# One core: attention's loads spread over a chunk, a selection matrix built on the chip, load rows of whole 64 bytes, the first chunks' exponents reordered

## The chip, the cores and the metric

The kernel runs on one core of one Trainium2 chip. The metric is device time in microseconds, and the time before is the median of three runs. A second, profiled execution of the same program gives the trace that the rows below are from.

## The reference

Three stages in a row: a gated linear attention over 768 steps (2 batches, 8 heads of 40), a mixture of 8 experts with the best 2 for each of 1536 tokens, and a two-layer network. All inputs and the result are float32. Cut to what matters:

```python
for t in range(S):                                     # attention, S = 768
    m_new = np.maximum(f_gate[:, :, t] + m, i_gate[:, :, t])
    f_stab = np.exp(f_gate[:, :, t] + m - m_new)
    i_stab = np.exp(i_gate[:, :, t] - m_new)
    m = m_new
    C = f_stab[..] * C + i_stab[..] * einsum('bhd,bhe->bhde', vt, kt)
    n = f_stab[..] * n + i_stab[..] * kt
    h = einsum('bhde,bhe->bhd', C, qt)
    y[:, :, t] = sigmoid(o_gate[:, :, t]) * h / max(abs(sum(n * qt)), 1)
# experts: x is (1536, 320)
noisy = x @ w_gate + log1p(exp(x @ w_noise)) * noise   # top 2 of 8, softmax of the two
out[tok] += w * (relu(x[tok] @ w1[e]) @ w2[e])         # w1 320x1024, w2 1024x320
# network
h = x @ w_in                                           # 320 -> 2048
out = (h * clip(h + 3, 0, 6) / 6) @ w_out
```

## The kernel before

The order of the work is written out by hand: each engine executes its instructions in the order in which the program gives them, and the loads are nearly all issued from SP, also in program order, so a load that has to wait holds back all that SP would issue after it.

**Attention** runs in 12 chunks of 64 steps. The exponents of the gates come first: a scan over time gives the running maximum `mt` (`scan`, L177), and `exponents` (L187) turns it into three bfloat16 parts that are written into the tile `RWG`, for chunks 0 and 1 and for 2 and 3 on 16 rows each (`first_exponents(0)` and `(1)`), for the others at once on 64 rows (`later_exponents`, L217, after `mt` was copied to another layout by a POOL transfer into `m64`). A bfloat16 tile `SEL` (128 x 8 x 2 x 64) holds a selection of rows and an identity; `expo` (L296) multiplies it with `RWG` on TensorE (PE) and ACT takes the exponential into `dd`; POOL then scales the keys with it (`kt`, L310). `cbt` is a small tile of constants in bfloat16, among them the identity that `warm` (L367) uses to keep PE busy on 512 columns.

One turn n of the loop (L1138) does, on PE: `inter(n)` (queries by the state `Sb`), `values(n)`, `state(n)`, `scores(n+2)`, the transposes of chunk n-1's result (`xpose`, L437, copied to `xT` by ACT), `expo(n+2)`, at some n `decays`, and the router's `logits(n-1)`, which need `xT`. DVE does `pmul(n+1)` (scores by `dd`), the new state, and the normalisation `norm_eg`, `norm_pv`; ACT the rest of it (`norm2`, 9 operations) and the output gates (`gate`, in two or three operations on two chunks). In turns 4 to 10 the steps of `route` (`go(r0)`, `go(r1)`) stand between them on DVE, which find the slots of the tokens; from them POOL gathers the first expert's tokens.

Loads of a turn: `load_qk(n+3)` (two halves of 192 KB), `load_kv(n+3)` (324 KB, tiles in four buffers), `load_on` (two chunks' output gates), the store `put(n-1)`, and in the turns that `WD` names a piece of expert weights (`w_load`, 512 or 640 KB, into one of four buffers of `RAW`). Each piece is later split into a high part by ACT (`w_hi`, turns in `WH`) and a low part by DVE (`w_lo`, turns in `WL`; for the third piece of an expert both parts go into one stacked tile, L693). `w_split` does the two and the next load; the list `WS` names the steps of the first units for it.

**The experts** are units of up to 416 tokens: 8 blocks f of L1 (8 matmuls, L937), relu on ACT, and L2 (L973 to L978), with a lag of two steps. `bg(i, f, ...)` and `bga` hang other work on step f of unit i. `xprep` turns gathered tokens into `XH` and `XL` (L874 to L877). The network's units follow the experts' in the same loop.

Of the kernel before, what the change touches and what calls it, by code (L numbers as in the profile page):

```python
# [25 lines left out]
NT = 12  # L26
# [8 lines left out]
RAWB = 4  # L35
WL = (0, 0, 0, 1, 1, 1)
WD = (0, 1, 1, 1, 0, 0, 1, 0, 1, 2)
WH = (0, 0, 1, 1, 1, 0, 0, 0, 1, 1)
SP = 4
SP2 = 4  # L40
SPI = 4
WARM = 8
XW = 384
# [3 lines left out]
VSPLIT = {}  # L47
WS = ((0, 2), (0, 3), (0, 4), (0, 5), (0, 7), (1, 2), (1, 3), (1, 4), (1, 6), (2, 1))
TROWS = CAP + 11 * 128
# [22 lines left out]
@with_exitstack  # L72
def mlstm_moe_mlp(ctx, tc, qk, kv, on, gf, gf4, sl, w1, w2, w_in, w_out, cf, cb, out):
    nc = tc.nc
# [13 lines left out]
    def bank(i):  # L88
        return (ps if i >= 4 else psd).tile([128, 512], F32, name=f"bank{i}")
# [19 lines left out]
    nc.sync.dma_start(gft, gf)  # L109
    cbt = const.tile([128, 528], BF, name="cbt")  # L110
    A.dma_start(cbt, cb)
# [3 lines left out]
    ltri, ones = cbt[:, 256:384], cbt[:, 384:512]  # L115
    sel16 = cbt[:, 512:528].rearrange("p (h b) -> p h b", b=B)

# [12 lines left out]
    def kv_part(n):  # L130
        kvt[n] = att.tile([128, H * (D + V1)], F32, name="kv", bufs=4)
        return kvt[n], kv[n]
# [5 lines left out]
    def load_kv(n, eng=nc.sync):  # L138
        eng.dma_start(*kv_part(n))
# [13 lines left out]
    load_qk(0, (A, nc.sync))  # L153
    nc.sync.dma_start(SEL, sl)
    load_kv(0, A)
# [21 lines left out]
    def scan(a, b):  # L177
        V.tensor_tensor_scan(mt[:, a + 1:b + 1], gft[:, 1, a:b], gft[:, 0, a:b], mt[:, a:a + 1] if a else neg, OP.add, OP.max)

    scan(0, 128)  # L180
# [43 lines left out]
    late = None  # L224
    cft = const.tile([128, 444], F32, name="cft")
    wgt = cft[:, 288:336].rearrange("p (k c) -> p k c", k=3)
# [102 lines left out]
    def inter(n, bp=5, two=itp):  # L329
        q = QK[n % 3]  # L330
        vv = kvt[n][:, DM:].rearrange("p (h d) -> p h d", h=8)
        pv = [t.rearrange("p (a c) -> p a c", a=4)
              for t in (bank(bp)[:, 0:4 * V1], wb[:, 320:320 + 4 * V1] if bp == 5 else bank(6)[:, 0:4 * V1])]
        it = two[:, :, 0:4 * V1].rearrange("p x (a c) -> p x a c", a=4)
        for p in range(4 if n else 0):
            for x in range(2):
                r = slice(64 * x, 64 * x + D)
                for b in range(B):
                    T.matmul(it[rows[b], x, p, :], q[r, p, 0, rows[b]], Sb[r, b ^ x, p, :], start=True, stop=True)
        y_ps[n] = (pv, it, vv)  # L340
# [18 lines left out]
    def values(n):  # L359
        pv, _, vv = y_ps[n]  # L360
        for p in range(4):
            for b in range(B):
                for x in range(2):
                    h, r = 4 * x + p, rows[b ^ x]
                    T.matmul(pv[x][rows[b], p, :], Pt[n][r, h, :], vv[r, h, :], start=True, stop=True)

    def warm(k):  # L367
        for _ in range(k):
            T.matmul(wb, identb, cbt[:, 0:512], start=True, stop=True)

# [62 lines left out]
    lgt, xT = {}, {}  # L433
    wb = bank(7)
    rt = {}
# [241 lines left out]

    def raw_load(src):
        j = len(loaded) % RAWB
        t = RAW[:, 1280 * j:1280 * j + 1280]  # L680
        for r0, r1, ap, w in src:
            o = t[r0:r1, 0:w]
            nc.sync.dma_start(o if len(ap.shape) == 2 else o.rearrange("p (f d) -> p f d", d=DM), ap)
        return t
# [115 lines left out]

    def w_load():
        if pos[0] < len(queue):
            loaded.append(raw_load(queue[pos[0]][0]))
            pos[0] += 1
# [309 lines left out]


    scan(128, S)
    G.dma_start(m64, bass.AP(tensor=mt.tensor, offset=mt.offset + 256, ap=[mt.ap[0], [128, 4], [1, 129]]))
    warm(WARM)
    expo(0)
    scores(0)  # L1120
    decays(0, 2)
    expo(1)
    scores(1)
    pmul(0)
    fe = first_exponents(1)
    next(fe)
    next(fe)
    pmul(1)
    for _ in fe:
        pass  # L1130

    def norm(n):
        norm_pv(n)
        norm2(n)
        if n:
            put(n)

    for n in range(NT - 2):  # L1138
        if n:
            pmul(n + 1)  # L1140
        if n == 1:
            norm(0)
        if n == 9:
# [3 lines left out]
        if n + 3 < NT:  # L1147
            load_qk(n + 3)
            load_kv(n + 3)
        if n in (0, 1, 3, 5, 7):  # L1150
            load_on(n + 2 + n % 2 if n else 2)
        if n > 1:
# [3 lines left out]
        if n and n % 2 == 0:  # L1156
            gate(n, 2)
        state(n)
        norm_eg(n)
        if n:  # L1160
            norm_pv(n)
        else:
            for _ in later_exponents():
                pass
        if n == 1:
            G.tensor_copy(adj, iota8)
            G.tensor_copy(iotab, iota128)
        for _ in range(WD[n] if n < len(WD) else 0):
            w_load()
        if n == 0:  # L1170
            for i in range(3):
                gate(0, i)
        elif n % 2:
            gate(n + 1, 0)
            gate(n + 1, 1)
# [3 lines left out]
        if n in (6, 8):  # L1179
            go(r0)  # L1180
        expo(n + 2)
        if n == 0:
            decays(2, 4)
        elif n in (2, 6):
            decays(n + 2, n + 6)
# [11 lines left out]
        if 4 <= n <= 8:  # L1197
            go(r0)
        w_hi(WH[n] if n < len(WH) else 0)
        w_lo(WL[n] if n < len(WL) else 0)  # L1200
# [68 lines left out]
    bg(0, 1, open_late)  # L1269
    for f in range(2):  # L1270
        bg(0, f, w_lo)
        bg(0, f, w_load)
    for f in (2, 4, 6):
# [86 lines left out]
def _arrays(inp):  # L1360
# [18 lines left out]
    kn, vn = [_np.concatenate([z[:, :, :4], _np.roll(z[:, :, 4:], 64, axis=1)], axis=2) for z in (kn, vn)]  # L1379
    kv = _np.concatenate([kn.reshape(NT, 128, -1), vn.reshape(NT, 128, -1)], axis=2)  # L1380
    on = nat(o)[:, :, halves].reshape(NT, 128, H * D).transpose(1, 0, 2)
# [23 lines left out]
    for r in range(48):  # L1405
        sel[r // 16 * 32 + r % 16, r % 2 * 4 + r % 8 // 2, r % 16 // 8] = 1.0
    sq = sel.copy()
    sq[:, 4:] = sel[:, 4:, ::-1]
    sl = sq[:, :, :, None] + mk[:, None, None, 64:]
    sl = sl.astype(ml_dtypes.bfloat16)  # L1410
    cb = _np.concatenate([cb, sel.reshape(128, 16).astype(ml_dtypes.bfloat16)], axis=1)
    ci = (_np.arange(NT)[None] * 128 + p[:, None]).astype(_np.int32)
    cf = _np.concatenate([cf, wg.reshape(128, 48), nz.reshape(128, 96), ci.view(_np.float32)], axis=1).astype(_np.float32)
    a = dict(qk=qk, kv=kv, on=on, gf=gf, gf4=gf4, sl=sl, w1=inp['moe_w1'], w2=inp['moe_w2'],
             w_in=bits(inp['moe2_w_in']).reshape(DM, 2, F).transpose(1, 0, 2).reshape(2 * DM, F), w_out=bits(inp['moe2_w_out']).reshape(2, 8, 128, DM).transpose(0, 2, 1, 3).reshape(256, 8 * DM), cf=cf, cb=cb)
# [17 lines left out]
```

## Time and profile before

| | |
|---|---|
| median of 3 runs | 507.71 us (507.58 to 509.29) |
| profiled execution: time | 507.86 us |
| profiled execution: span, first to last instruction | 506.1 us |
| PE busy | 479.2 us, 95% of the span, 4554 matmuls |
| PE weight loads | 437.5 us, 86% |
| DVE / ACT / POOL busy | 333.8 (66%) / 237.8 (47%) / 94.7 us (19%) |
| granted PE clock, mean | 0.919 |
| moved by DMA | 91.00 MB, 180 GB/s over the span |

The page of the profile gives busy times and shares over the whole execution; the stages differ, so stretches of it are read by windows. Attention takes about the first 90 us, the experts run to about 310 us and the network to the end. A row of the timeline says when an instruction, or a run of like ones, began, how long it took, on which engine and line, what it wrote and read, and in brackets how long the engine had been idle before it and what ended that. "issue" there means that nothing in the profile explains the wait. Rows of the DMA view count the packets that a queue began in a stretch.

### The profile page before, as it was taken

Reading aid. Unit: us, or ns where it says so; the run is one execution under the profiler, and the core shown is the slowest. Engines: PE = TensorE matmul, PEld = TensorE weight load, DVE = VectorE, ACT = ScalarE, POOL = GpSimd, SP = SyncE. Lnnn points to the kernel's source line nnn. Section 1 sums busy time; section 2 is a strip of 40 time slices with the busy share of each in tenths; the row PEclk is TensorE's granted clock in tenths of the full one; section 3 lists DMA queues with packets and bytes.
Section 4 is the critical chain, followed back from the end, with each engine's and each line's share of the span. In section 5 each row is a group of like instructions: output and inputs, shape, how many; then the busy total and the mean of one; then the engine's idle time right before and its main releaser. Section 6 shows DMA issues by size and latency. Waiting matters only on the chain. (4 is left out here: it accounts for less than half of the span.)

```text
span 506.1 us, 11541 instructions
## 1 busy us (share of the span) xinstructions
PE 479.2 (95%) x4554; PEld 437.5 (86%) x4554; DVE 333.8 (66%) x823; ACT 237.8 (47%) x495; POOL 94.7 (19%) x117
## 2 busy tenths in 40 slices
PE   5799897989999999999999999899999999999996
PEld 3587785889999999999999998788888989999995
DVE  6756787698658787878788863676885434353534
ACT  3677665355446454545454633555553334333331
POOL 3323122305032010202010024784001000000000
PEclk9555555699999999999999999999999999999999
DMA  8978673477827998979887694979214300020111
GB/s 202 264 214 225 179 204 132 130 221 239 262 82 278 282 310 261 337 248 310 259 297 229 216 305 137 301 213 275 104 53 116 145 1 0 1 52 1 27 27 52
DMA packets 41193, 91.00 MB, mean 180 GB/s; under 512 B 4817, under 2 KB 23505, under 8 KB 41137
## 3 DMA queue, kind: packets, MB, share of 16 engines
q1 hardware_dynamic: 34736, 69.52, 44.2%
q0 software_dynamic: 5728, 19.73, 12.8%
q10 hardware_dynamic: 672, 0.99, 0.7%
q8 instruction: 36, 0.59, 0.5%
q14 instruction: 21, 0.16, 0.1%
HBM read 67.42 MB, written 22.68 MB: 178 GB/s over the span
## 5 line engine op out<-in xcount | busy, mean ns | idle before, releaser
L952 DVE SCALAR_TENSOR_TENSOR r<-r,bank 128x512 f32<-128x512 f32 (+1 forms) x56 | 34.2, 610 | 84.2 <-ACT r L951 82.3
L951 ACT ACTIVATE r<-bank,cft 128x512 f32<-128x512 f32 (+1 forms) x56 | 35.0, 626 | 99.1 <-PE bank L937 86.7
L940 ACT ACTIVATE hb<-bank 128x416 fp32r<-128x416 f32 (+2 forms) x80 | 35.7, 446 | 90.0 <-PE bank L937 77.9
L937 PE MATMUL bank<-XH,SB 128*128 128x416 f32 (+3 forms) x280 | 75.8, 341 | 0.3 <-PEq L1037 0.3
L937 PE MATMUL bank<-XL,SB 128*128 128x416 f32 (+3 forms) x192 | 67.1, 349 | 1.6 <-DVE XL L876 1.6
L973 PE MATMUL bank<-SB,hb 128*128 128x320 f32 x192 | 62.3, 324 | 3.2 <-ACT hb L924 2.8
L973 PE MATMUL bank<-SA,hb 128*128 128x320 f32 x192 | 60.8, 317 | 0.0
L864 POOL DMA_INDIRECT XG<-Xd,idx x32 | 34.7, 1083 | 138.9 <-PE bank L874 108.5
L975 PE MATMUL bank<-SB,hb 128*128 128x320 f32 x192 | 59.9, 312 | 0.1
L975 PE MATMUL bank<-SA,hb 128*128 128x320 f32 x192 | 59.3, 309 | 0.1
L974 PE MATMUL bank<-SA,hb 128*128 128x320 f32 x192 | 59.2, 308 | 0.0
L974 PE MATMUL bank<-SB,hb 128*128 128x320 f32 x192 | 59.2, 308 | 0.0
L937 PEld LDWEIGHTS bank<-XH,SB 128*128 128x128 f32 x280 | 50.3, 188 | 4.6 <-issue 0.6
L937 PE MATMUL bank<-XH,SA 128*128 128x416 f32 (+2 forms) x200 | 51.3, 329 | 0.0
L973 PEld LDWEIGHTS bank<-SB,hb 128*128 128x128 f32 x192 | 36.2, 188 | 5.3 <-ACT hb L924 3.8
L937 PE MATMUL bank<-XL,SA 128*128 128x416 f32 (+2 forms) x120 | 39.4, 329 | 0.2 <-DVE XL L876 0.2
L937 PEld LDWEIGHTS bank<-XL,SB 128*128 128x128 f32 x192 | 36.2, 188 | 3.9 <-DVE XL L876 1.9
L937 PEld LDWEIGHTS bank<-XH,SA 128*128 128x128 f32 x200 | 36.5, 196 | 1.6 <-ACT XH L875 0.3
L975 PEld LDWEIGHTS bank<-SB,hb 128*128 128x128 f32 x192 | 36.0, 188 | 1.4 <-DVE hb L925 1.3
L973 PEld LDWEIGHTS bank<-SA,hb 128*128 128x128 f32 x192 | 36.1, 188 | 1.1
L974 PEld LDWEIGHTS bank<-SA,hb 128*128 128x128 f32 x192 | 36.2, 188 | 0.9
L946 DVE SCALAR_TENSOR_TENSOR hb<-bank,hb 128x32 fp32r<-128x32 f32 x64 | 12.0, 188 | 37.6 <-ACT hb L940 37.5
(225 smaller groups left out, 1063.2 us busy)
## 6 DMA issues: line engine op xcount, KB each, us to landing
raw<-in_w_dram SPq DMA_DIRECT2D x18, 640.0 KB
raw<-in_w_dram SPq DMA_DIRECT2D x18, 512.0 KB
craw<-in_w_in_dram SPq DMA_DIRECT2D x8, 640.0 KB
craw<-in_w_out_dram SPq DMA_DIRECT2D x8, 640.0 KB
raw<-in_w_dram SPq DMA_DIRECT2D x18, 256.0 KB
qk<-in_qk_dram SPq DMA_DIRECT2D x23, 192.0 KB
Yd<-yo SPq DMA_DIRECT2D x24, 160.0 KB
kv<-in_kv_dram SPq DMA_DIRECT2D x11, 324.0 KB
```

The lines of the kernel that those rows point to most:

```text
L864: G.indirect_dma_start(out=XG[0:n, (u.xo + i) % 4, :], out_offset=None, in_=Xd[0:CUT[u.i] * 128] if early else Xd[:, :], in_offset=bass.In ...
L937: T.matmul(p, a, b, start=(i == 0), stop=(i == 7))
L940: A.activation(hb[:, 0:N], p, AF.Relu)
L946: V.scalar_tensor_tensor(hb[:, N:N + u.tail], p[:, o:N], 0.0, hb[:, o:N], OP.max, OP.subtract)
L951: A.activation(r, p, AF.Relu, bias=three)
L952: V.scalar_tensor_tensor(r, r, 6.0, p, OP.min, OP.mult)
L973: T.matmul(p, h, wh, start=s, stop=False)
L974: T.matmul(p, h, wl, start=False, stop=False)
L975: T.matmul(p, hb[:, lo:lo + n], wh, start=False, stop=t)
```

## The change

- `SEL` is no longer loaded (256 KB). Two pairs of matmuls on 512 columns build it in two banks, from the identity, 16 new columns of `cbt` and its 64-column identity, and ACT copies each bank to the tile. `warm` runs 4 times in place of 8, right behind them.
- Rows of `kv` go from 2592 to 2624 bytes, of `cbt` from 1056 to 1088, of `cft` from 1776 to 1792.
- `kv` has three buffers in place of four; `load_kv(n+3)` and `load_on` move from before `norm2` to behind `state(n)`.
- `w_load` moves to behind `expo(n+2)`, and a POOL memset of one element of the buffer stands before it, which the load has to wait for. `w_hi` moves from the end of a turn to before `state`. `WD`, `WH` and `WL` name other turns; one load comes in turn 9 ahead of the others, one behind the last chunk's normalisation.
- The scan is cut in two at step 256. Five steps of chunk 2 and 3's exponents go ahead of `pmul(0)`, the rest ahead of `pmul(1)`, and the scan of the remaining steps with the transfer to `m64` behind it. In turn 0 `norm_pv(0)` and `pmul(2)` come ahead of `later_exponents`.
- At the change to the experts, 3 and 2 warming matmuls are added around the first `xprep`, one `w_lo` goes ahead of unit 0, and one split goes from unit 0 to unit 1.

```diff
-WL = (0, 0, 0, 1, 1, 1)
-WD = (0, 1, 1, 1, 0, 0, 1, 0, 1, 2)
-WH = (0, 0, 1, 1, 1, 0, 0, 0, 1, 1)
+KW = 656
+WL = (0, 0, 0, 1, 1, 0, 0, 0, 1)
+WD = (0, 0, 1, 1, 0, 0, 1, 0, 1, 1)
+WH = (0, 0, 0, 1, 1, 0, 0, 1, 0, 1)
-WARM = 8
+WARM = 4
-WS = ((0, 2), (0, 3), (0, 4), (0, 5), (0, 7), (1, 2), (1, 3), (1, 4), (1, 6), (2, 1))
+WS = ((0, 2), (0, 3), (0, 4), (0, 6), (1, 0), (1, 2), (1, 3), (1, 4), (1, 6), (2, 1))
...
-    cbt = const.tile([128, 528], BF, name="cbt")
+    cbt = const.tile([128, 544], BF, name="cbt")
...
-    sel16 = cbt[:, 512:528].rearrange("p (h b) -> p h b", b=B)
+    sel16, selq = [cbt[:, c:c + 16].rearrange("p (h b) -> p h b", b=B) for c in (512, 528)]
...
-        kvt[n] = att.tile([128, H * (D + V1)], F32, name="kv", bufs=4)
+        kvt[n] = att.tile([128, KW], F32, name="kv", bufs=3)
...
     load_qk(0, (A, nc.sync))
-    nc.sync.dma_start(SEL, sl)
     load_kv(0, A)
...
+    for i in range(2):
+        p = bank(5 + i)
+        hs = slice(4 * i, 4 * i + 4)
+        T.matmul(p, identb, selq[:, hs, :, None].to_broadcast([128, 4, B, 64]), start=True, stop=False)
+        T.matmul(p, identb, eyeb[:, None, :].to_broadcast([128, 8, 64]), start=False, stop=True)
+        A.copy(SEL[:, hs].rearrange("p h b t -> p (h b t)"), p)
+    warm(WARM)
...
-    cft = const.tile([128, 444], F32, name="cft")
+    cft = const.tile([128, 448], F32, name="cft")
...
-    def raw_load(src):
+    def raw_load(src, held):
         j = len(loaded) % RAWB
         t = RAW[:, 1280 * j:1280 * j + 1280]
+        if held:
+            G.memset(t[0:1, 0:1], 0.0)
...
-    scan(128, S)
-    G.dma_start(m64, bass.AP(tensor=mt.tensor, offset=mt.offset + 256, ap=[mt.ap[0], [128, 4], [1, 129]]))
-    warm(WARM)
+    scan(128, 256)
     expo(0)
     scores(0)
     decays(0, 2)
     expo(1)
     scores(1)
+    fe = first_exponents(1)
+    for _ in range(5):
+        next(fe)
     pmul(0)
-    fe = first_exponents(1)
-    next(fe)
-    next(fe)
-    pmul(1)
     for _ in fe:
         pass
+    pmul(1)
+    scan(256, S)
+    G.dma_start(m64, bass.AP(tensor=mt.tensor, offset=mt.offset + 256, ap=[mt.ap[0], [128, 4], [1, 129]]))
...
     for n in range(NT - 2):
-        if n:
+        if n > 1:
             pmul(n + 1)
         if n == 1:
-            norm(0)
+            norm2(0)
...
             load_qk(n + 3)
-            load_kv(n + 3)
-        if n in (0, 1, 3, 5, 7):
-            load_on(n + 2 + n % 2 if n else 2)
         if n > 1:
             norm2(n - 1)
         if n:
             put(n - 1)
         if n and n % 2 == 0:
             gate(n, 2)
+        w_hi(WH[n] if n < len(WH) else 0)
         state(n)
+        if n + 3 < NT:
+            load_kv(n + 3)
+        if n in (0, 1, 3, 5, 7):
+            load_on(n + 2 + n % 2 if n else 2)
+        if n == 9:
+            w_load()
         norm_eg(n)
-        if n:
-            norm_pv(n)
-        else:
-            for _ in later_exponents():
-                pass
+        if n == 0:
+            for i in range(3):
+                gate(0, i)
+        norm_pv(n)
...
-        for _ in range(WD[n] if n < len(WD) else 0):
-            w_load()
-        if n == 0:
-            for i in range(3):
-                gate(0, i)
-        elif n % 2:
+        if n % 2:
             gate(n + 1, 0)
             gate(n + 1, 1)
...
         expo(n + 2)
+        for _ in range(WD[n] if n < len(WD) else 0):
+            w_load(True)
         if n == 0:
             decays(2, 4)
+            pmul(2)
+            for _ in later_exponents():
+                pass
...
-        w_hi(WH[n] if n < len(WH) else 0)
         w_lo(WL[n] if n < len(WL) else 0)
...
     norm(n)
+    w_load()
     norm_eg(n + 1)
     norm(n + 1)
     open_psd()
+    spare = bank(2)
+    warm(3, spare)
     xprep(units[0], 0, 5)
     xprep(units[0], 1, 3)
     xpose(n, 4)
+    warm(2, spare)
+    w_lo()
...
-    for f in range(2):
-        bg(0, f, w_lo)
-        bg(0, f, w_load)
+    bg(0, 0, w_load)
+    bg(0, 0, w_hi)
+    bg(0, 1, w_lo)
+    bg(0, 1, w_load)
```

## Rows read from the trace of the kernel before

**Rows 1.** Windows: busy us by engine (instructions), PE clock, DMA share, GB/s.
```profile
core 0: us, PE busy (x) PEld busy (x) DVE busy (x) ACT busy (x) POOL busy (x), PEclk, DMA share, GB/s
5.00:10.00 5.00, 4.09 (x63) 1.94 (x63) 3.24 (x9) 1.00 (x2) 0.54 (x1) 1.00 1.03 248
30.00:40.00 10.00, 10.00 (x316) 8.75 (x318) 5.24 (x14) 8.16 (x23) 2.27 (x3) 0.50 0.79 255
...
90.00:100.00 10.00, 9.77 (x95) 8.56 (x94) 6.18 (x15) 2.99 (x8) 3.96 (x7) 0.65 0.47 134
...
150.00:200.00 50.00, 50.00 (x313) 48.24 (x312) 40.62 (x82) 24.77 (x41) 8.09 (x8) 1.00 0.83 271
```

**Rows 2.** Timeline, PE, attention: start, length, what ran [idle before it].
```profile
21.76 0.80 PE L294 MATMUL s4p<-qk 40*64 40x64 f32 x18 [1.12 <-issue]
...
41.67 1.13 PE L294 MATMUL s4p<-qk 40*64 40x64 f32 x30 [1.15 <-issue]
...
76.77 0.48 PE L294 MATMUL s4p<-qk 40*64 40x64 f32 x3 [1.04 <-issue]
...
83.63 0.51 PE L349 MATMUL itp<-kv,kt 64*40 64x41 f32 x16 [1.71 <-issue]
```

**Rows 3.** Instruction queue: packets, MB, share; whole span, then 39.3:39.4, then 81.4:81.5.
```profile
q8 instruction: 36, 0.59, 0.5%
...
q8 instruction: 1, 0.02, 60.4%
...
q8 instruction: 1, 0.02, 60.3%
```

**Rows 4.** Timeline, SP's load issues in chunk 9.
```profile
77.13 0.87 SPq L683 DMA_DIRECT2D raw<-in_w_dram  x2
```

**Rows 5.** SP's load queue, 17.8 to 18.8 us: packets, MB, share of 16 engines.
```profile
q1 hardware_dynamic: 135, 0.31, 102.2%
```

**Rows 6.** Timeline, PE: inter of chunks 3 and 4.
```profile
31.71 1.36 PE L339 MATMUL itp<-Sb,qk 40*64 40x41 f32 x29
...
37.79 1.09 PE L339 MATMUL itp<-Sb,qk 40*64 40x41 f32 x32
```

**Rows 7.** DMA issues of the first 10 us: what, count, KB each.
```profile
SEL<-in_sl_dram SPq DMA_DIRECT2D x1, 256.0 KB
```

**Rows 8.** Timeline, PE, the head: warming and the first exponents.
```profile
3.94 3.60 PE L369 MATMUL bank<-cbt 128*128 128x512 bf16 x8 [3.94 <-DMA cbt<-in_cb_dram]
...
8.45 0.41 PE L300 MATMUL bank<-SEL,RWG 128*64 128x512 bf16 x2 [0.91 <-DMA SEL<-in_sl_dram]
```

**Rows 9.** Timeline, DVE and PE, chunks 5 and 6.
```profile
53.91 1.27 DVE L693 SCALAR_TENSOR_TENSOR SA<-sth,cft,raw 128x1024 fp32r<-128x1024 f32 x1
...
55.84 1.13 PE L294 MATMUL s4p<-qk 40*64 40x64 f32 x32 [1.45 <-DVE P L317]
```

**Rows 10.** Timeline, POOL, ACT and PE, chunk 3.
```profile
31.33 0.74 POOL L310 TENSOR_TENSOR kt<-kv,dd 128x320 f32<-128x320 f32 x1 [2.14 <-ACT dd L305]
...
31.54 1.05 ACT L687 CAST SA<-raw 128x1024 fp32r<-128x1024 f32 x1
...
34.51 0.73 ACT L147 ACTIVATE ont<-ont 128x640 f32<-128x640 f32 x1
...
36.33 0.48 ACT L442 COPY xT<-bank 128x384 f32<-128x384 f32 x1 [0.32 <-PE bank L440]
...
37.33 0.52 PE L453 MATMUL s4p<-cft,xT 128*32 128x16 f32 x24
```

**Rows 11.** Timeline, DVE and PE, chunk 10 and the first gathered tokens.
```profile
83.51 0.43 DVE L593 TENSOR_TENSOR yo<-yo,cft 128x256 f16<-128x256 f16 x1
...
84.77 0.42 PE L604 MATMUL s4p<-yo,yo 128*128 128x32 f16 x8
...
89.48 1.56 PE L874 MATMUL bank<-cft,XG 128*128 128x128 f32 x6
```

**Rows 12.** Timeline, PE, the first L1 of unit 1.
```profile
111.40 0.39 PE L937 MATMUL bank<-XL,SB 128*128 128x256 f32 x1 [1.63 <-DVE XL L876]
```

More of the change, by code (lines that the diff above doesn't have):

```diff
@@ L72, in mlstm_moe_mlp @@
 @with_exitstack
-def mlstm_moe_mlp(ctx, tc, qk, kv, on, gf, gf4, sl, w1, w2, w_in, w_out, cf, cb, out):
+def mlstm_moe_mlp(ctx, tc, qk, kv, on, gf, gf4, w1, w2, w_in, w_out, cf, cb, out):
     nc = tc.nc
@@ L178, in scan, with warm @@
         V.tensor_tensor_scan(mt[:, a + 1:b + 1], gft[:, 1, a:b], gft[:, 0, a:b], mt[:, a:a + 1] if a else neg, OP.add, OP.max)
+    wb = bank(7)
+    def warm(k, p=None):
+        for _ in range(k):
+            T.matmul(wb if p is None else p, identb, cbt[:, 0:512], start=True, stop=True)
+    for i in range(2):
[5 more added lines that the diff above has]
+    warm(WARM)
     scan(0, 128)
@@ L330, in inter @@
         q = QK[n % 3]
-        vv = kvt[n][:, DM:].rearrange("p (h d) -> p h d", h=8)
+        vv = kvt[n][:, DM:DM + H * V1].rearrange("p (h d) -> p h d", h=8)
         pv = [t.rearrange("p (a c) -> p a c", a=4)
@@ L365, in values @@
                     T.matmul(pv[x][rows[b], p, :], Pt[n][r, h, :], vv[r, h, :], start=True, stop=True)
-    def warm(k):
-        for _ in range(k):
-            T.matmul(wb, identb, cbt[:, 0:512], start=True, stop=True)
     xt, yt = {}, {}
@@ L433, in mlstm_moe_mlp @@
     lgt, xT = {}, {}
-    wb = bank(7)
     rt = {}
@@ L799, in mlstm_moe_mlp, with w_load @@
     pos = [0, 0]
-    def w_load():
+    def w_load(held=False):
         if pos[0] < len(queue):
-            loaded.append(raw_load(queue[pos[0]][0]))
+            loaded.append(raw_load(queue[pos[0]][0], held))
             pos[0] += 1
@@ L1379, in _arrays @@
     kn, vn = [_np.concatenate([z[:, :, :4], _np.roll(z[:, :, 4:], 64, axis=1)], axis=2) for z in (kn, vn)]
-    kv = _np.concatenate([kn.reshape(NT, 128, -1), vn.reshape(NT, 128, -1)], axis=2)
+    kv = _np.concatenate([kn.reshape(NT, 128, -1), vn.reshape(NT, 128, -1), _np.zeros((NT, 128, 8), _np.float32)], axis=2)
     on = nat(o)[:, :, halves].reshape(NT, 128, H * D).transpose(1, 0, 2)
@@ L1408, in _arrays @@
     sq[:, 4:] = sel[:, 4:, ::-1]
-    sl = sq[:, :, :, None] + mk[:, None, None, 64:]
-    sl = sl.astype(ml_dtypes.bfloat16)
-    cb = _np.concatenate([cb, sel.reshape(128, 16).astype(ml_dtypes.bfloat16)], axis=1)
+    cb = _np.concatenate([cb] + [z.reshape(128, 16).astype(ml_dtypes.bfloat16) for z in (sel, sq)], axis=1)
     ci = (_np.arange(NT)[None] * 128 + p[:, None]).astype(_np.int32)
-    cf = _np.concatenate([cf, wg.reshape(128, 48), nz.reshape(128, 96), ci.view(_np.float32)], axis=1).astype(_np.float32)
-    a = dict(qk=qk, kv=kv, on=on, gf=gf, gf4=gf4, sl=sl, w1=inp['moe_w1'], w2=inp['moe_w2'],
+    cf = _np.concatenate([cf, wg.reshape(128, 48), nz.reshape(128, 96), ci.view(_np.float32), cf[:, :4]], axis=1).astype(_np.float32)
+    a = dict(qk=qk, kv=kv, on=on, gf=gf, gf4=gf4, w1=inp['moe_w1'], w2=inp['moe_w2'],
              w_in=bits(inp['moe2_w_in']).reshape(DM, 2, F).transpose(1, 0, 2).reshape(2 * DM, F), w_out=bits(inp['moe2_w_out']).reshape(2, 8, 128, DM).transpose(0, 2, 1, 3).reshape(256, 8 * DM), cf=cf, cb=cb)
```

## The prediction

> **What bounds the kernel now.** The windows come first [rows 1]: TensorE (PE) is busy all 10 us of 30 to 40 and all 50 us of 150 to 200, so the kernel is PE-bound. But the granted clock is 0.50 (1.2 GHz) in the one and 1.00 (2.4 GHz) in the other. It is 1.00 in 5 to 10, and 0.65 over 90 to 100, where it comes back. Attention, about 15 to 90 us, runs at the low level, and PE fills even that. A microsecond gained or lost on PE before the experts start moves everything behind it, since nothing there is full except PE. So I list what PE waits for in attention.
>
> The timeline of PE has gaps put down to nothing ("issue"), the four longest of 1.12, 1.15, 1.04 and 1.71 us [rows 2]. The instruction queue explains them. Its 36 packets are 16 KB each, and PE runs 4554 matmuls with as many weight loads: 9108 / 36 = 253 instructions to a packet. Counted along the kernel, the gaps lie at multiples of about that. The packets that begin in the tenths at 39.3 and 81.4 us last 0.97 and 0.96 us (60.4% and 60.3% of 16 times 0.1 us) [rows 3], and PE resumes at 41.67 and 83.63: 1.4 and 1.3 us behind their ends. The later one begins only when two weight loads issued at 77.13 [rows 4] have drained. So a packet of code waits behind loads in flight, and PE stops if that takes longer than its last 250 instructions. Four smaller stalls only stretch a group of matmuls: 29 take 1.36 us in chunk 3, where chunk 4's 32 take 1.09 [rows 6]; by the same reading they come to 1.25 us.
>
> **The change, part by part.** The profiled execution took 507.86 us (span 506.1 and 1.8 around it), 0.15 above the median, 507.71. The sum starts from 507.86.
>
> *SEL made on the chip.* This removes a 256 KB load [rows 7] at the head of the queue. Loads run at 248 GB/s with the DMA engines full in 5 to 10 us [rows 1], so all behind it lands 0.262 MB / 248 GB/s = 1.06 us earlier, the code packet that ends the gap at 21.76 too. The first exponents wait 0.91 us for SEL [rows 8]. Four new matmuls of 512 columns take the place of four of the eight warming ones, at 0.45 us each (3.60 / 8), so PE's early activity and its instruction count stay; two ACT copies of about 0.6 us fall before RWG is ready. Take -1.05; ends 0 (something else, such as the output gates, lands last) and -1.5.
>
> *Exponents in another order.* The scan is cut, and chunk 2's exponents go ahead of pmul(0). That frees expo(2), but PE next meets a code boundary, which goes by the loads. In return norm_pv(0) and pmul(2) stand on DVE ahead of later_exponents, behind gates that ACT does when their load has come. Chunk 2's inter has some 4 us of slack over Sb. Take 0, ends -0.4 and +1.
>
> *Rows of whole 64 bytes.* In 17.8 to 18.8 us, mostly rows of kv, 0.31 MB moved at a share of 1.022, 303 GB/s [rows 5]. Full engines in 150 to 200 move 271 / 0.83 = 326. If the longer rows reach that, a load of 0.33 MB gains 0.08 us, and four of them in the head 0.3. Take 0, ends 0 and -0.3. The Trainium skill (DMA: Bandwidth & Descriptors, How a descriptor splits into AXI transactions) says that transactions start at 256-byte boundaries, so 2624-byte rows are cut up no better than 2592; by that it is 0 as well, and no row of before shows an aligned kv.
>
> *Loads spread out.* kv moves behind state and a weight load behind expo, held by a POOL memset that runs after kt. On SP the memset's wait stands ahead of the next chunk's qk, whose use is over 6 us away. Following the code boundaries (PE's order is kept) with the new issue times, most packets are asked for when little is queued. The one that ends at 41.67 still meets a weight load, qk and kv. I take the four small stalls and 0.15 of 1.15: -1.4; ends 0 and -2.4.
>
> *Conversions moved.* The stacked piece's subtraction (1.27 us on DVE) leaves the end of chunk 5, where it stood ahead of the pmul that held PE for 1.45 us [rows 9]. Take -1.2. It now stands at the end of chunk 8.
>
> w_hi moves from a chunk's end to its middle, and here ACT can be late: each piece is converted one chunk after its load was let go. In chunk 3, kt ends at 31.33 + 0.74 = 32.07 [rows 10]. Two loads from 77.13 drained by 81.4, so one takes half of 4.3 us, and some 1.2 more until it can be used: 3.0 to 3.3. ACT then converts at 35.1 for 1.05, does two gates of 0.74, and copies xT in 0.48: 38.1, where PE took the logits at 37.33. That is 0.8 late. Chunk 7 repeats it (0.9), chunk 4 has no gates there (0.1). Take +1.8; ends 0 and +8.9.
>
> *The last two chunks.* Gaps of 1.04 and 1.71 us go by the queues. But next is DVE: routing's one-hot product ends at 83.94, and PE takes it at 84.77 [rows 11], so only 0.83 is free, and the subtraction moved to chunk 8 adds 1.27 to this chain. With chunk 9's own slack I keep -0.3; ends -2.75 and +0.5.
>
> *Warming at the units' start.* Five matmuls of 0.45 us are 2.25. Three stand where PE would wait for the gather (4.3 us lie between the one-hot product's end and the first gathered tokens [rows 11], and PE's work between is 2.7 us), so nothing; two delay the first unit by some 0.4, since XL is late there anyway. In return the clock may rise sooner: in 90 to 100 it averages 0.65, that is, 7 us at half speed. Take -0.2; ends +1.7 and -1.7.
>
> *Splits moved in unit 0.* One w_lo goes ahead of unit 0, and one split behind unit 1's XL, each up to 1.48 us on a DVE that is full there. The 1.63 us that PE waits for XL [rows 12] should go: -1.5, ends 0 and -1.63.
>
> Sum: -1.05 - 1.4 - 1.2 + 1.8 - 0.3 - 0.2 - 1.5 = -3.85, so 504.0 us.
>
> **Rivals.** *The conversion waits for nothing*, and the code packets all get through: -1.8, -1.0 for the gap at 41.67 and -0.8 more in the last chunks: 500.4. For it speaks that a load by itself meets an empty queue in chunk 3.
>
> *The code gaps stay*, because loads are no less dense where packets are asked for, or because they are not the cause: the terms -1.4 and -0.3 fall away, 505.7. Against it stands that PE resumes at nearly the same distance behind both packets. The Trainium skill (Runtime: NRT & Kernel Launch, Instruction fetch mechanics) has code fetched in 16 KiB blocks with the cost "mostly hidden". The trace agrees on the block and not on the hiding: 1.71 us.
>
> *Slower: ACT stands behind a weight load.* In order, it holds the gates, xT and dd behind a w_hi whose piece has not come. If a held load needs 5 us from POOL's release, because it shares the queue with qk and kv, chunks 3, 4 and 7 lose 2.8, 2.0 and 3.0 us, and chunk 9 loses 1.1 beyond what DVE's chain hides: 8.9 in place of 1.8, 511.1. It decides from about 4.3 us on (no gain left); over 0.5% slower from 4.9. For it: two loads together took 4.3 us to drain. Against: in chunks 3 and 7 the queue should be empty.
>
> **How the numbers follow.** Forecast 504.0 (own range 502.3 to 505.2): 0.47. All gaps gone: 0.18. Gaps stay: 0.25. ACT behind the loads: 0.10. A measurement can tell about 0.5% from no change, so faster is below 505.2 and slower above 510.2. Faster: 0.44 of the forecast, 0.18, and 0.07 from the gaps that stay, where other terms do better: 0.69. Slower: 0.10, same: 0.21. The range, 500.3 to 507.8, leaves out the slow rival and the far ends of the gain.
>
> **What would show it.** The wait for SEL is gone and the gap of 21.76 ends near 20.7; the gaps at 76.77 and 83.63 are gone, with a wait for DVE in the place of the second; no 1.45 us wait in chunk 6, none for XL at unit 1. ACT's conversion in chunks 3 and 7 begins on a DMA, and logits there wait for xT. The prediction is wrong if ACT never waits for raw, if gaps stand behind code packets as before, or if the clock falls or rises at another place.

## The result and the profile after

The changed kernel is slower: 510.02 us median against 507.39 for the kernel before in the same session, ratio 1.0075 (95% interval 1.0052 to 1.0098). Forecast were 504.0 us and a range of 500.3 to 507.8. The profiled execution took 513.24 us (span 511.4), 3.2 above its median, so its waits are read for where they lie; what they are worth is read from ratios of medians. Executions of one kernel spread by about 1% to either side, and chips differ too (the kernel before had medians from 503 to 507.5), so every ratio below is to the kernel before on the same chip.

The timeline of PE in the kernel after (start, length, what ran, idle before it and its cause; P is what `pmul` writes on DVE, the scores times `dd`):

```profile
7.39 0.41 PE L314 MATMUL bank<-SEL,RWG 128*64 128x512 bf16 x2
12.00 0.50 PE L363 MATMUL itp<-kv,kt 64*40 64x41 f32 x30 [1.15 <-DVE P L331]
...
20.74 0.79 PE L308 MATMUL s4p<-qk 40*64 40x64 f32 x17 [1.47 <-issue]
27.30 1.14 PE L308 MATMUL s4p<-qk 40*64 40x64 f32 x32 [0.72 <-DVE P L331]
39.20 0.52 PE L462 MATMUL s4p<-cft,xT 128*32 128x16 f32 x24 [2.25 <-ACT xT L451]
46.33 0.38 PE L462 MATMUL s4p<-cft,xT 128*32 128x16 f32 x24 [1.47 <-ACT xT L451]
49.33 1.13 PE L308 MATMUL s4p<-qk 40*64 40x64 f32 x32 [1.21 <-DVE P L331]
69.08 0.53 PE L462 MATMUL s4p<-cft,xT 128*32 128x16 f32 x24 [3.72 <-ACT xT L451]
83.95 0.52 PE L462 MATMUL bank<-cft,xT 128*32 128x16 f32 x24 [2.29 <-ACT xT L451]
87.83 0.51 PE L363 MATMUL itp<-kv,kt 64*40 64x41 f32 x15 [1.15 <-issue]
```

Much of what the change was to remove is gone. The first exponents wait for no `SEL` and begin at 7.39, where [rows 8] had 8.45. Of the gaps of [rows 2], those at 41.67 and 76.77 are not there; the first ends at 20.74, near the 20.7 that was forecast, but is longer (1.47), and the last is 1.15. The 1.45 us wait for P of [rows 9] is gone, and one of 1.21 us stands a chunk earlier. What is new is that the logits wait for `xT` in chunks 3, 4, 7 and 9: 2.25 + 1.47 + 3.72 + 2.29 = 9.73 us, where [rows 10] shows none. In the timeline of ACT the cause stands ahead of the gates and the copy to `xT` each time:

```profile
36.33 1.04 ACT L698 CAST SA<-raw 128x1024 fp32r<-128x1024 f32 x1 [2.75 <-DMA raw<-in_w_dram]
44.86 1.04 ACT L698 CAST SA<-raw 128x1024 fp32r<-128x1024 f32 x1 [2.56 <-DMA raw<-in_w_dram]
66.21 1.04 ACT L703 CAST sth<-raw 128x1024 fp32r<-128x1024 f32 x1 [4.76 <-DMA raw<-in_w_dram]
80.87 1.26 ACT L698 CAST SA<-raw 128x1280 fp32r<-128x1280 f32 x1 [2.24 <-DMA raw<-in_w_dram]
```

The conversion of a weight piece (`w_hi`) waits for its load, and the gates and the copy to `xT` stand behind it in ACT's order. The loads' way to there, from the timelines of POOL and SP: the release and the issue for the pieces of chunks 3 and 7, and the issue alone for those of chunks 4 and 9:

```profile
31.92 0.09 POOL L691 MEMSET raw<- 1x1 f32 x1
32.04 0.33 SPq L694 DMA_DIRECT2D raw<-in_w_dram  x1
...
40.51 0.33 SPq L694 DMA_DIRECT2D raw<-in_w_dram  x1
...
59.74 0.09 POOL L691 MEMSET raw<- 1x1 f32 x1
59.85 1.22 SPq L694 DMA_DIRECT2D raw<-in_w_dram  x2
...
76.57 0.39 SPq L694 DMA_DIRECT2D raw<-in_w_dram  x1
```

From the issue on, ACT could begin after 36.33 - 32.04 = 4.3 us in chunk 3 and after 66.21 - 59.85 = 6.4 in chunk 7 (one piece in two transfers); the same subtraction gives 4.4 and 4.3 for the casts at 44.86 and 80.87.

### The profile page after: what moved, and what is told of

Same layout as the page of the kernel before. It is cut to its first block, busy times and chain, and to the rows that moved or that the text cites. A ratio compares the mean times of both kernels' runs of the same rounds, so it can differ in the third digit from the quotient of the medians.

```text
span 511.4 us, 11554 instructions
## 1 busy us (share of the span) xinstructions
PE 477.7 (93%) x4559; PEld 434.7 (85%) x4559; DVE 334.1 (65%) x824; ACT 238.4 (47%) x497; POOL 94.2 (18%) x122
## 5 line engine op out<-in xcount | busy, mean ns | idle before, releaser
L875 POOL DMA_INDIRECT XG<-Xd,idx x32 | 33.5, 1048 | 141.8 <-PE bank L885 110.1
L986 PEld LDWEIGHTS bank<-SA,hb 128*128 128x128 f32 x192 | 36.0, 188 | 1.5 <-DVE hb L954 1.1
L984 PEld LDWEIGHTS bank<-SA,hb 128*128 128x128 f32 x192 | 36.1, 188 | 1.1
L985 PEld LDWEIGHTS bank<-SA,hb 128*128 128x128 f32 x192 | 36.2, 188 | 0.9
```

What stands on the lines that cost most here:

```text
L875: G.indirect_dma_start(out=XG[0:n, (u.xo + i) % 4, :], out_offset=None, in_=Xd[0:CUT[u.i] * 128] if early else Xd[:, :], in_offset=bass.In ...
L984: T.matmul(p, h, wh, start=s, stop=False)
L985: T.matmul(p, h, wl, start=False, stop=False)
L986: T.matmul(p, hb[:, lo:lo + n], wh, start=False, stop=t)
```

## The experiments

Theory: what ACT waits for is the landing of a held load, and the other parts gain as forecast or less. Rivals: a cast in the middle of a chunk costs whether its load has come or not; or the waits only hide others.

**The conversion back at the turn's end** (kernel after, one line moved; label e1_hi_end).

```diff
-        w_hi(WH[n] if n < len(WH) else 0)
         state(n)
...
+        w_hi(WH[n] if n < len(WH) else 0)
         w_lo(WL[n] if n < len(WL) else 0)
```

> The kernel after, with one line moved back: each piece's conversion on ACT (w_hi) stands at the turn's end again, where the kernel before has it, ahead of w_lo. Loads, holds and all else stay as in the kernel after. Theory (ACT, in order, stands behind a held weight load, and PE waits for xT): the four waits of PE for xT in chunks 3, 4, 7 and 9 (2.25 + 1.47 + 3.72 + 2.29 = 9.73 us) go, some 1.5 us of it come back as waits for dd or P at the next turn's start, so about 8 us less than the kernel after: ratio to the kernel before 0.989 to 0.995. Rival (the order in the middle of a chunk costs by itself, the wait for raw only hides another wait, such as DVE's or a code packet's): the waits for xT get another name, and the ratio stays at 1.003 to 1.010.

Measured: 0.9965 (0.9940 to 0.9989), so 0.8 to 1.1% less than the kernel after with its two ratios, 1.0041 (below) and 1.0075; that is 4 to 5.5 us where 8 was expected. ACT waits for no raw in attention, PE for `xT` 0.4 us. Some of it came back as expected, as waits for P (4.65 us in sum against 3.68). In chunk 4 `w_lo` on DVE waits for the later cast, the next `pmul` stands behind it, and PE behind that:

```profile
45.23 1.23 DVE L699 TENSOR_TENSOR SA<-raw,SA 128x1024 fp32r<-128x1024 f32 x1 [1.75 <-ACT SA L698]
46.38 0.68 DVE L331 TENSOR_TENSOR P<-s4p,dd 128x512 f32<-128x512 f32 x1
...
47.12 1.13 PE L308 MATMUL s4p<-qk 40*64 40x64 f32 x32 [1.24 <-DVE P L331]
```

In this run the DMA view has the time from issue to landing (last column), which the page of the kernel before has not; for the four held pieces, let go in turns 2, 3, 6 and 8, and then for a load at the units' start:

```profile
raw<-in_w_dram SPq DMA_DIRECT2D x1, 512.0 KB, 4.2
raw<-in_w_dram SPq DMA_DIRECT2D x1, 512.0 KB, 5.4
raw<-in_w_dram SPq DMA_DIRECT2D x2, 256.0 KB, 3.9
raw<-in_w_dram SPq DMA_DIRECT2D x1, 640.0 KB, 5.3
...
raw<-in_w_dram SPq DMA_DIRECT2D x1, 512.0 KB, 4.0
```

Eight of the traces have landing times. Ahead of 100 us their weight loads took 3.5 to 6.3 us for 256 KB (these go out in pairs, and the median of a pair is given), 3.5 to 6.8 for 512 KB and 4.0 to 5.7 for 640 KB. So the size does not order them, and half the bytes do not land in half the time. How much is a fixed time and how much goes by the loads beside it, these rows do not tell apart.

**The conversion in the middle, in the kernel before** (the same line moved the other way; loads unheld, label e2_before_hi_mid).

```diff
+        w_hi(WH[n] if n < len(WH) else 0)
         state(n)
...
-        w_hi(WH[n] if n < len(WH) else 0)
         w_lo(WL[n] if n < len(WL) else 0)
```

> The kernel before, with only the conversion (w_hi) moved from a turn's end to its middle, ahead of state. Loads stay unheld and where they were. Theory (the wait is for the load, not for the place): in the kernel before a piece is asked for ahead of the gates of the turn before, so it has landed; ACT waits for no raw, and the time is that of the kernel before within 1 us: ratio 0.998 to 1.002. Rival (a cast of 1.04 us in the middle delays gates, xT and dd whether its load has come or not): five casts at 0.5 to 1 us each on PE's path, ratio 1.005 to 1.010, with waits of PE for xT or dd but none of ACT for raw.

Measured: 0.9996 (0.9972 to 1.0021). The theory's time holds, its "ACT waits for no raw" does not: even unheld, three of five pieces are late, by 0.9 to 1.8 us, and PE waits 1.85 us for `xT` in sum.

```profile
33.65 1.04 ACT L687 CAST SA<-raw 128x1024 fp32r<-128x1024 f32 x1 [0.96 <-DMA raw<-in_w_dram]
41.38 1.05 ACT L692 CAST sth<-raw 128x1024 fp32r<-128x1024 f32 x1 [1.76 <-DMA raw<-in_w_dram]
```

So the place of the cast alone costs nothing that can be told (some 1.2 us to either side); what costs is the place together with a load that comes late for it.

**Loads one turn earlier** (kernel after, conversions left in the middle; labels e4_loads_earlier and, on another chip, e9_loads_earlier).

```diff
-WD = (0, 0, 1, 1, 0, 0, 1, 0, 1, 1)
+WD = (0, 1, 1, 0, 0, 1, 0, 1, 1)
```

> The kernel after, with each held weight load of turns 2, 3, 6, 8 and 9 asked for one turn earlier (turns 1, 2, 5, 7, 8), at the same place in the turn; the conversions stay in the middle of turns 3, 4, 7 and 9. Theory (ACT stands behind the load, which took 4.3 to 6.4 us from POOL's release until ACT could begin): with some 6.4 us more in hand every piece has landed, ACT waits for no raw and PE for no xT; 7 to 9 us less than the kernel after, ratio 0.988 to 0.995. Rival (the conversion in the middle is the cost, not the load): ratio 1.003 to 1.010, PE still waits for xT or dd. If code gaps come back because loads are denser, one or two of about 1 us, that shows as issue gaps, not as waits for xT.

> The same kernel as e4 (the kernel after, held loads one turn earlier), again, beside the three edits of it that follow. Theory (what ACT waited for is gone, and the rest of the change gives 2 to 3 us): ratio to the kernel before 0.992 to 0.997, no wait of PE for xT over 0.6 us. Rival (the 0.9945 was a matter of that chip): ratio 0.997 or more.

Measured: 0.9945 (0.9922 to 0.9969) and 0.9959 (0.9929 to 0.9989). The four casts wait for nothing:

```profile
32.58 1.04 ACT L698 CAST SA<-raw 128x1024 fp32r<-128x1024 f32 x1
...
39.33 1.03 ACT L698 CAST SA<-raw 128x1024 fp32r<-128x1024 f32 x1
...
59.05 1.04 ACT L703 CAST sth<-raw 128x1024 fp32r<-128x1024 f32 x1
...
72.44 1.25 ACT L698 CAST SA<-raw 128x1280 fp32r<-128x1280 f32 x1
```

One tuple takes the change from 0.4 to 0.75% slower than the kernel before to about 0.5% faster, with the hold, and with the order of all work on ACT, unchanged.

**The kernel after again, and without the hold** (labels e5_after, e6_no_hold; same chip).

```diff
-            w_load(True)
+            w_load()
```

> The kernel after, unchanged, on the same chip as the next runs, so that what its waits for xT cost can be read against one set of runs of the kernel before. Theory (ACT behind the held loads): PE waits for xT in chunks 3, 4, 7 and 9 again, some 8 to 10 us in all, and the ratio to the kernel before is 1.005 to 1.010, that is 10 us of waits less some 6 us that the rest of the change and a clock that rises in the pauses give. Rival (the waits of the first trace were of that one execution): under 5 us of waits and a ratio under 1.003.

> The kernel after with the POOL memset ahead of the held loads left out (w_load(True) made w_load()): a load is issued where SP comes to it, behind kv of the same turn. In the trace of the kernel after SP had issued kv (and the gates) at 29.7, 35.4, 56.6 and the held load only at 32.0, 40.5, 59.9: 2.3, 5.1 and 3.3 us later. Theory (the landing takes 4 to 6 us wherever it starts, and the hold adds its wait to it): the loads land at about 35, 40.5 and 62 by the old times, ACT waits 0 to 1.5 us in each place, PE for xT 0 to 2 us in all; ratio 0.995 to 1.000. Rival (the queue is what is slow: unheld, a load only shares it with kv in place of qk and lands no earlier): ACT still waits 2 us and more in three chunks, ratio 1.003 to 1.010.

Measured: 1.0041 (1.0014 to 1.0069) for the kernel after, with waits of 1.74, 1.28, 3.28 and 4.30 us for `xT`, 10.6 in sum; 0.9966 (0.9941 to 0.9990) without the hold. Its first two loads go out at 29.34 and 35.47, and of the waits for raw (12.3 us in the kernel after) 3.5 us are left:

```profile
33.61 1.04 ACT L698 CAST SA<-raw 128x1024 fp32r<-128x1024 f32 x1 [0.48 <-DMA raw<-in_w_dram]
...
42.09 1.04 ACT L698 CAST SA<-raw 128x1024 fp32r<-128x1024 f32 x1 [2.25 <-DMA raw<-in_w_dram]
...
60.30 1.04 ACT L703 CAST sth<-raw 128x1024 fp32r<-128x1024 f32 x1 [0.76 <-DMA raw<-in_w_dram]
```

The piece of chunk 4 came later than expected: its load went out right behind kv's (34.55) and could be used 6.6 us after its issue (42.09 - 35.47), where the held one of the kernel after took 4.4. So the hold's 2 to 5 us are not all gained, but most are. With the conversion moved, the hold removed or the load advanced, one at a time, the loss goes; that settles the cause.

The two runs are from one chip, so their traces show what the waits for `xT` are worth. Ahead of unit 0 PE's waits of 0.15 us and more come to 18.0 us in e5 and to 10.2 in e6: 10.95 for `xT` (the four and one of 0.35) are gone, but 5.9 are put down to issue in place of 4.2, and 1.9 to other operands in place of 0.3. Of these 7.8 us unit 0 begins 4.2 sooner (91.69 for 95.92), close to the 3.8 of the ratio. Most of the rest had come back through the clock in e5: in 70 to 80 us 0.84 is granted (0.50 in e6), inter of 32 takes 0.68 us there in place of 1.09, and from 72.51 to 79.15 PE needs 4.9 us without its waits, where e6 needs 7.6 for the same groups.

```profile
73.61 0.68 PE L353 MATMUL itp<-Sb,qk 40*64 40x41 f32 x32
```

Whether the pauses bring the clock back is not shown; it is one execution of each.

**SEL alone** (kernel before with the matrix made on the chip and four warming matmuls fewer, label e3_sel; the edit is that of the change).

> The kernel before, with only the selection matrix made on the chip (four matmuls of 512 columns and two ACT copies, four warming matmuls fewer, no 256 KB load). Theory (the forecast's term): all loads of the head land 1.05 us earlier, the first exponents wait for no SEL, the gap of PE at 21.76 moves to about 20.7; ratio 0.997 to 0.999. Rival (another load or a code packet sets the head, and nothing is gained): ratio 1.000, with the gap of PE put at the same place or the time before it filled by another wait.

Measured: 0.9975 (0.9951 to 0.9999), 0 to 2.5 us, with the forecast's 1.05 in it. The wait for `SEL` is gone, but in this execution a gap of 1.68 us stands at 18.57 in place of the one at 21.76, and PE ran at the low level from the first exponents on, as the lengths of the rows show (the last section comes back to them):

```profile
7.65 0.64 PE L306 MATMUL bank<-SEL,RWG 128*64 128x512 bf16 x2
...
8.76 1.13 PE L300 MATMUL s4p<-qk 40*64 40x64 f32 x32
...
18.57 0.17 PE L255 MATMUL bank<-cbt,RWG 128*64 128x8 bf16 x1 [1.68 <-issue]
```

So this trace cannot show where the gap goes.

**Load rows alone** (kernel before with the padded rows, label e8_rows).

> The kernel before with only the load rows made whole multiples of 64 bytes (kv 656 in place of 648 columns, the two constant tiles 544 and 448). Theory (rows of 2624 bytes move no faster than 2592): kv lands as late as in the kernel before, within 0.2 us, ratio 0.999 to 1.002. Rival (whole 64-byte rows gain, up to the rate of full engines, 326 in place of 303 GB/s): 0.3 us at the head and shorter kv landings, ratio 0.998 to 0.9995.

Measured: 0.9984 (0.9957 to 1.0011). Both expectations lie in the interval and this trace has no landing times, so it stays open whether the rows gain 0.3 us or nothing.

**The exponents' order undone** (on the kernel with earlier loads, labels e7_exponents_undone and, beside e9, e12_exponents_undone).

```diff
-    scan(128, 256)
+    scan(128, S)
...
-    for _ in range(5):
-        next(fe)
     pmul(0)
-    for _ in fe:
-        pass
+    next(fe)
+    next(fe)
     pmul(1)
...
-            pmul(2)
```

> The kernel with the loads one turn earlier (e4), with the first chunks' exponents put back in the order of the kernel before (one scan from 128 on, pmul(0) ahead of them, norm of chunk 0 in turn 1, no pmul(2) ahead of the later exponents). Theory (the forecast's 0 for this part was too low a cost: PE's wait for P of 1.5 us in chunk 1 and 0.5 us in chunk 2 are the new order's): these fall to about 0.5 us in all, chunk 3 begins 0.5 to 1.5 us sooner, ratio 0.991 to 0.994 where e4 had 0.9945. Rival (the code gaps and chunk 2's slack take it, as forecast): chunk 3 begins within 0.4 us of e4's, ratio 0.994 to 0.996.

> The same kernel as e7 (e4 with the first chunks' exponents in the order of the kernel before), beside e9 this time. Theory (the new order costs PE 1 to 1.5 us of waits for P in chunks 1 and 2): waits for P before 30 us fall from 2.0 to about 0.5 us, ratio 0.001 to 0.003 below e9's. Rival (the waits are exchanged for a gap behind a code packet later in the same chunks, as e7's 3.12 us at 37.4 suggests): the sum of gaps put down to issue is 2 us and more above e9's, ratio equal to e9's or above it.

Measured: 0.9961 (0.9936 to 0.9987) and 0.9906 (0.9871 to 0.9941), with 0.9945 and 0.9959 for the other order: not told apart. In the traces the waits for P ahead of 30 us fall to 0.53, as the theory had it, and gaps put down to issue take their place, as the rival had it, for instance in e7:

```profile
12.24 0.50 PE L363 MATMUL itp<-kv,kt 64*40 64x41 f32 x30 [0.53 <-DVE P L331]
16.59 0.17 PE L263 MATMUL bank<-cbt,RWG 128*64 128x8 bf16 x1 [1.52 <-issue]
...
37.36 0.42 PE L316 MATMUL bank<-RWG,SEL 128*128 128x64 bf16 x5 [3.12 <-issue]
```

**No warming at the units' start** (e9 without its five matmuls, label e10_no_warm).

```diff
-    warm(3, spare)
...
-    warm(2, spare)
```

> e9 without the five warming matmuls at the units' start (three ahead of the first split, two behind the last transposes). Theory (forecast: they cost and give back about the same, -0.2 us): the first unit starts 0.5 to 1.5 us sooner and the granted clock rises up to 3 us later behind its start, ratio within 0.002 of e9's. Rival (the earlier rise of the clock is a gain of its own, since in the kernel before it came 5.4 us behind the unit's start and here 1.5 us): without them 1.5 to 2.5 us slower, ratio 0.003 to 0.005 above e9's.

Measured: 0.9954 (0.9928 to 0.9981), e9's ratio. Windows of 92 to 96 us, first with the warming (e9), then without:

```profile
92.00:94.00 2.00, 2.00 (x39) 1.83 (x38) 0.40 (x2) 1.57 (x3) 0.52 (x1) 1.00 0.86 260
94.00:96.00 2.00, 2.00 (x17) 2.00 (x16) 1.56 (x3) 0.38 (x2) 0.00 (x0) 1.00 0.45 108
```
```profile
92.00:94.00 2.00, 2.00 (x32) 1.74 (x32) 0.42 (x1) 0.69 (x2) 0.81 (x1) 0.50 0.44 152
94.00:96.00 2.00, 2.00 (x35) 1.84 (x34) 0.34 (x1) 1.63 (x3) 0.24 (x1) 0.76 1.07 275
```

The granted clock does rise some 4 us sooner, and the time is the same within the intervals.

**The first units' conversions undone** (e9 with the order of the kernel before in unit 0; labels e11_unit0_splits, e13_unit0_splits, and e14_both_undone with the exponents undone too).

```diff
-WS = ((0, 2), (0, 3), (0, 4), (0, 6), (1, 0), (1, 2), (1, 3), (1, 4), (1, 6), (2, 1))
+WS = ((0, 2), (0, 3), (0, 4), (0, 5), (0, 7), (1, 2), (1, 3), (1, 4), (1, 6), (2, 1))
...
+        if n == 9:
+            w_hi()
...
     warm(2, spare)
-    w_lo()
...
-    bg(0, 0, w_load)
-    bg(0, 0, w_hi)
-    bg(0, 1, w_lo)
-    bg(0, 1, w_load)
+    for f in range(2):
+        bg(0, f, w_lo)
+        bg(0, f, w_load)
```

> e9 with the conversions at the first units put back as in the kernel before: a fifth piece converted at the end of turn 9, no w_lo ahead of unit 0, unit 0's splits in the old list. Theory (the wait for XL at unit 1 was exchanged for waits behind the same full DVE): PE's wait for XL comes back at 1 to 1.6 us, the waits of 0.2 to 0.6 us for hb and yo between 100 and 125 us go, ratio within 0.002 of e9's. Rival (forecast: -1.5 us for this part): 1.5 us slower, ratio 0.003 above e9's, waits of PE in 100 to 125 us 1.5 us more in sum.

> The same kernel as e11 (held loads one turn earlier, the first units' conversions in the order of the kernel before), since its first ratio, 0.9895, had an interval of 0.0040 to either side. Theory (the new order of the conversions costs in unit 0, where a cast of 1.26 us stands on ACT ahead of an activation that PE and DVE go on from: from unit 0's first matmul to the first store of unit 3 e11's trace had 79.4 us, e4's and e9's 80.3 and 81.8): 79 to 80 us again, ratio 0.988 to 0.993. Rival (e11's were good executions, the two orders are alike): 80 to 82 us, ratio 0.994 to 0.997.

> e13 with the first chunks' exponents in the order of the kernel before as well, so that of the change there remain SEL on the chip, the load rows, the spread loads one turn earlier and the warming. Theory (both orders cost something: 1 us and more each): ratio 0.985 to 0.991, 0.002 to 0.004 below e13's, PE's waits for P before 30 us at 0.5 us. Rival (the exponents' order is exchanged for code gaps, as in e7 and e12, whose gaps of 2.15 and 3.12 us were put down to issue): ratio equal to e13's within 0.002 or above it.

Measured: 0.9895 (0.9855 to 0.9935), 0.9954 (0.9922 to 0.9985) and 0.9934 (0.9903 to 0.9966): all are faster than the kernel before, none is told from e9 by its time. The traces differ more clearly. From unit 0's first matmul to unit 3's first store e11 takes 168.31 - 88.93 = 79.4 us, e13 79.0 and e14 79.6; the eight traces with the new order and the warming take 79.7 to 82.2, 81.0 in the mean. The first two rows are e9's activations around the moved cast, the third is e11's:

```profile
92.02 1.26 ACT L698 CAST SA<-raw 128x1280 fp32r<-128x1280 f32 x1
93.18 0.39 ACT L951 ACTIVATE hb<-bank 128x256 fp32r<-128x256 f32 x1
```
```profile
92.61 0.38 ACT L951 ACTIVATE hb<-bank 128x256 fp32r<-128x256 f32 x1 [0.41 <-PE bank L948]
```

Counted from unit 0's first matmul the second relu is 4.0 us in for e9 and 3.7 for e11. PE's wait for XL falls (1.62 us in e11, 0.42 in e9), but others come up at once, here in e9 (`hb` is what relu writes):

```profile
109.59 0.41 PE L986 MATMUL bank<-SA,hb 128*128 128x320 f32 x1 [0.41 <-DVE hb L954]
110.98 0.35 PE L613 MATMUL bank<-yo,yo 128*128 128x32 f16 x8 [0.54 <-DVE yo L602]
113.45 0.42 PE L984 MATMUL bank<-SB,hb 128*128 128x320 f32 x1 [0.63 <-DVE yo L1017]
...
120.58 0.52 PE L885 MATMUL bank<-cft,XG 128*128 128x128 f32 x3 [1.66 <-DMA XG<-Xd,idx]
```

The longest is not one for DVE, but for gathered tokens (XG). It differs from execution to execution: none in e4, 1.71 us in e12, and with the old order none in e11 and e13, 0.64 in e14. All of PE's waits of 0.15 us and more in the stretch come to 2.0 to 3.9 us, mean 2.9, in the eight traces and to 1.9, 1.9 and 2.5 in the three; so they are somewhat under half of the difference in length, and the rest of it stays open.

## Why the prediction was wrong, step by step

**The conversions moved: mis-sized, and the cause of the sign.** The step had the mechanism: ACT in order, `xT` behind the held load, chunks 3, 4, 7 and 9. It took 3.0 to 3.3 us from POOL's release until the piece can be used; the trace shows 4.3 to 6.4. With these in place of 3.0 the step's own sum gives 2.1, 1.5 and 4.3 us of waiting in chunks 3, 4 and 7, and 2.25, 1.47 and 3.72 were measured; so it was this size that was off. The error is in the half: two loads issued together drained in 4.3 us [rows 4], and I gave one of them half. The same pair, issued at 77.01 in e3, whose trace has landing times, took 4.0 us from issue to landing in the median, and the first of the two 3.6:

```profile
raw<-in_w_dram SPq DMA_DIRECT2D x2, 512.0 KB, 4.0
```

So one of two takes nearly as long as the two together, and in the fuller chunks longer still. A page would have led to the same place: the Trainium skill (DMA: Bandwidth & Descriptors, Anatomy of one DMA) gives, for the gpsimd path, about 2.0 us fixed and bytes / 436e3, an estimate of 3.2 us for 512 KB. The landings here, on SP's path, are 0.8 us longer at the units' start in e1 and up to 3.6 longer in attention (6.8, in e4), so the measurement decides. "In chunks 3 and 7 the queue should be empty" was wrong too: `qk` was issued right behind (what that cost is not shown).

In chunk 9 the sum had nothing, since DVE's chain was to hide the wait. It was 2.29 us; without it PE waits there 0.5 to 0.9 us for DVE's one-hot product (0.48 at 82.23 in e4, 0.76 at 83.10 in e6), so that much of it was hidden and the rest was not. In place of +1.8 the waits were 9.73 us, with 2.8, 2.0, 3.0 and 1.1 in the slow rival and 2.25, 1.47, 3.72 and 2.29 measured. That rival, priced at 511.1 and given 0.10, is what happened, from the mechanism and the place it named; its deciding point, 4.3 us, was just reached by the smallest of the four. I weighed it too low: the only row on a load's duration spoke for it, and half of that row was my assumption. That its time fits as well is in part luck: the waits cost less than its 8.9 us, and the other parts gave less than 5.65.

Taking the wait out in the three ways gives back 0.75% (hold removed, same chip) to 1.3% of the time (loads earlier, against the larger ratio of the kernel after), 3.8 to 6.6 us, and not 9.7. The pair e5 and e6 shows where the difference goes: to other waits that come in their place, and to the clock.

**The other terms without ACT's** came to -5.65; e4 and e9, where ACT waits for no load, measured -0.41 to -0.55%, 2 to 3 us.

- *SEL*: -1.05 forecast, the wait gone, -1.3 with an interval of 1.2: right as far as it can be told.
- *Loads spread*: -1.4 forecast. The sum of PE's gaps put down to issue ahead of 92 us is 5.97, 8.24, 8.30 and 8.15 in the four traces with the old loads (before, e2, e3, e8), and 3.6 to 6.1, mean 4.6, in the eight with held loads and the new order of exponents. That is 3 us less, but not by the loads alone: with the loads held and the old order of exponents (e7, e12, e14) it is 8.05, 5.54 and 6.30, mean 6.6, some 1 us less than 7.7, the mean of the four. Without the hold it is 5.9, one trace. So the gaps get shorter, as the reason has it, and what the loads are worth cannot be told from -1.4. That the gaps are code that waits behind loads had no run of its own, nor had `kv`'s three buffers and its later place.
- *P in chunk 6*: -1.2 forecast, about 0 measured. The wait of [rows 9] is gone, but behind 30 us the waits for P add up to 0.7 to 2.1 us in the traces with the change, 1.1 to 2.3 in those without: when one pmul is on time, the next late one shows.
- *Exponents*: 0 forecast, and the ratios do not tell the two orders apart. In the traces it is an exchange: 0.7 to 2.6 us of waits for P ahead of 30 us against some 2 us of gaps put down to issue.
- *Warming*: about 0 in time (e10), as forecast. In the traces the stretch from unit 0's first matmul to unit 3's first store is shorter with it, 79.3 against 80.7 us in the old order of conversions (three traces, four) and 81.0 against 81.6 in the new (eight, one); e10's time shows nothing of that, so a small gain stays open.
- *Splits in unit 0*: -1.5 forecast. The wait for XL fell by 1.2 of 1.62, and the stretch grew by 1.7 (81.0 against 79.3). The prediction itself said that DVE is full there: the waits for `hb` and `yo` on DVE came up in its place (0.41, 0.54 and 0.63 in e9), and the longer wait for gathered tokens. The cast on ACT ahead of a relu is 0.3 us of it at the second relu.
- *Last chunks*: -0.3 forecast. The gap at 83.63 of 1.71 us is 1.15 at 87.83, but the wait for `xT` of 2.29 covers what it would have given.

**What bounds the kernel** was read rightly: attention's waits move all behind it. Unit 0 begins at 97.69 and 95.92 in the two traces of the kernel after, and at 88.9 to 92.1 in all others.

## What to carry over

Moving a use earlier, or a load nearer to its use, is safe only by the landing time of one load, measured from issue to use in the same stretch; that time must not be got by dividing the time of several. An engine that works in order should convert nothing in the middle of a chunk that is not known to have landed; one turn more between load and use cost nothing here and brought all of the loss back. Where PE waits for one thing after another, removing one wait is worth what the next waits leave, not its length.

## What was not expected of the hardware

The granted clock of the records can be wrong for a stretch. In e3 the windows of 10 to 30 us show 1.00:

```profile
10.00:20.00 10.00, 7.92 (x221) 6.48 (x222) 8.03 (x23) 4.22 (x10) 3.31 (x6) 1.00 0.83 223
20.00:30.00 10.00, 9.73 (x275) 7.80 (x270) 5.92 (x17) 7.03 (x23) 3.45 (x7) 1.00 0.85 233
```

but its 32 matmuls of scores take 1.13 us at 8.76 and 1.14 at 14.13, the length that goes with the 1.2 GHz level in the other traces, where e4 takes 0.69 at 8.53. The starts say the same: the next group begins 1.06 us later in e3 (9.82) and 0.62 in e4 (9.15). The Trainium skill (TensorE: Matmul & The Clock Gate, Part 1) warns that the recorded events of this clock are unreliable; this run agrees. The length of a known group is the better witness.

In some executions the clock also comes back for a few us within attention, each time at another place (in e4 and e6 it does not, from 20 us on): in the kernel after the inter of chunk 5 takes 0.68 us at 46.64, where [rows 6] has 1.09 for the same 32, and in e2 a window shows it:

```profile
70.00:80.00 10.00, 6.17 (x243) 5.15 (x244) 7.23 (x42) 7.83 (x21) 1.48 (x2) 0.84 0.66 233
```

There a gap of 3.83 us put down to issue stood at 76.43, the longest seen ahead of unit 0, and that execution (501.18 us) was still the shortest of its kernel's twelve. The gap at that boundary in turn 9 is 1.04 us in [rows 2], 3.83 here, and 0.35 in e10, so one trace of the kernel before is not enough to price such a gap.
